# One emission order for all stages of a Sinkhorn-attention, Fourier and MLP kernel, computed by an engine model, with a contiguous K eviction

## The chip, the cores and the metric

One Trainium2 chip, one core. The metric is the device time of one execution in microseconds (us), as the median of several runs. The profiles come from single executions; their span is about 2 us shorter than the device time. Engines: PE is TensorE, DVE is VectorE, ACT is ScalarE, POOL is GpSimd, SP is SyncE. TensorE's clock can be granted in part; 1.00 is full speed, and stretches at 0.5 are called cold. The heads are worked on in pairs ("head pair"), so 4 batches of 8 heads make 16 of them.

## The reference, cut to what matters

```python
# q, k, v: (4 batches, 8 heads, 768, 64) fp32; sort_net: (4, 8, 8, 8)
# moe_w_ch1: (512, 2048), moe_w_ch2: (2048, 512) fp32
P = sort_net
for _ in range(5):                       # Sinkhorn, 8x8 for each batch and head
    P = exp(P - max_row(P)); P = P / sum_row(P); P = P / sum_col(P)
k_sorted = einsum('bhij,bhjcd->bhicd', P, k_blocks)      # mixes 8 blocks of 96 rows
v_sorted = einsum('bhij,bhjcd->bhicd', P, v_blocks)
attn = softmax(q_block @ k_sorted_block.T / 8) @ v_sorted_block   # in each block
x = attn as (4, 768, 512)
u = x + real(fft(fft(x, axis=1), axis=2))
ch = relu(layernorm(u) @ w_ch1) @ w_ch2
out = u + ch
```

The kernel works in fp16 with fp32 accumulation. It writes the softmax as exp(s) - 1 plus a constant part and the Fourier transform as matmuls with cosine and sine tables; one row of it goes through a small fp32 "row path" with a table of its own. The MLP is the larger part of the matmul work.

## The kernel before

The stages were emitted by hand, in an order that mixes batches, so that the MLP of one batch stands beside the attention of another:

```python
    v_mean(0); v_cast(0); attn(0); a_path(0); a_rows(0); a_rows(1); fft_ln(0)
    load_v(1, [nc.sync, nc.sync])        # V of batches 2 and 3
    make_bdk(1); attn(1); fft_ln(1)
    v_mean(1); v_cast(1); v_mix(1); a_path(1)
    mlp(0)
    ...                                  # batches 2 and 3 likewise
    mlp(2); mlp(3)
```

K is mixed on TensorE and evicted by one cast to each of two engines. The mixed rows go out in their natural order, so that neighbouring values of the source land 12 bytes apart:

```python
            dst = ks[:, :, 0:BLK].rearrange("p i (c r) -> p r i c", r=6)[
                :, 3 * half:3 * half + 3]
            src = ps.rearrange("p r (i c) -> p r i c", c=16)
            if half == 0:
                nc.scalar.copy(dst, src)             # L436
            else:
                nc.vector.tensor_copy(dst, src)      # L438
        qr = wt([128, 6, 2, D], F16, "qr", 1)
        nc.vector.tensor_copy(                       # L440: waits for Q's load
            qr, q16[:, 2 * hl:2 * hl + 2].rearrange("p h r d -> p r h d"))
```

The softmax here doesn't subtract the row's maximum and nothing guards it: scores larger than these inputs give would overflow.

## Time and profile before

| | before |
|---|---|
| device time, median | 411.4 us (409.1 to 412.1, 3 runs; a fourth came later) |
| TensorE busy | 316.2 us, 77% of 408.5 |
| first attention scores | 49.1 us |
| first attention times V | 60.3 us |
| first MLP matmul | 121.1 us |

The page of the kernel before. The digits are the busy tenths of 40 slices of 10.2 us each; PEclk is the granted clock, DMA the busy share of the 16 DMA engines. In the stretch view further down this share can pass 1; about 1 and above is read here as full. GB/s counts bytes as they land, after the cast:

```profile
span 408.5 us, 6064 instructions
PE 316.2 (77%) x2452; PEld 185.1 (45%) x2452; DVE 212.2 (52%) x449; ACT 165.7 (41%) x298; POOL 55.7 (14%) x146
PE   0009896686084889989799889798888979979996
PEclk9999997568567999999999999899899989999999
DMA  8989943604030541100101560001000000010202
```

TensorE does nothing in the first three slices, is thin and cold (clock 0.5 to 0.8) in slices 7 to 13, and is dense from 140 us on. The same by stretches, in the stretch view (start and end; length; busy us and instructions of each engine; granted clock; DMA share; GB/s):

```profile
0.00:30.00 30.00, 0.00 (x0) 0.00 (x0) 10.68 (x35) 9.20 (x15) 22.72 (x30) 1.00 0.97 241
30.00:60.00 30.00, 27.65 (x210) 19.80 (x210) 13.26 (x22) 11.77 (x19) 0.75 (x1) 1.00 0.92 206
60.00:100.00 40.00, 28.10 (x267) 20.33 (x268) 26.00 (x55) 17.51 (x28) 2.36 (x3) 0.66 0.39 77
100.00:140.00 40.00, 19.49 (x151) 10.60 (x150) 30.80 (x61) 8.46 (x15) 8.99 (x28) 0.70 0.15 37
140.00:340.00 200.00, 178.55 (x1486) 101.65 (x1484) 119.36 (x257) 95.24 (x176) 18.24 (x71) 0.97 0.16 34
```

Who waits for whom, from the lists of waits of TensorE and VectorE (engine, tile and line, what it waited for: total us, times, longest):

```profile
PE pf_193 L265 <- DVE pdup_189 L256: 30.0, 1, 30.0
PE pf_933 L605 <- DVE un_931 L600: 12.1, 1, 12.1
...
DVE qr_266 L440 <- DMA q_86<-in_q_dram: 14.2, 1, 14.2
```

The first 30 us are a queue fault: VectorE's copy of Q (L440) waits 14.2 us for its load, and the Sinkhorn rounds stand behind it, though they need nothing of Q. GpSimd's timeline (start, length, operation) shows when the weights are loaded:

```profile
2.19 0.75 POOL L138 DMA_DIRECT2D q_86<-in_q_dram  x1
...
22.29 0.74 POOL L219 DMA_DIRECT2D w1sb<-in_moe_w_ch_dram  x1
23.02 1.16 POOL L220 DMA_DIRECT2D w2sb<-in_moe_w_ch_dram  x1
49.79 0.75 POOL L138 DMA_DIRECT2D q_137<-in_q_dram  x1 [25.61 <-DVE qr_518 L440]
```

They are issued at 22.3 us, because memsets stand in front of them in GpSimd's queue (from 2.9 us on, with two loads between them; one memset takes 6.9 us), and, against the program's text, ahead of batch 1's Q, which has to wait for a free buffer.

The K eviction is one line of the groups (busy us of the group, mean ns of one):

```profile
L436 ACT CAST ksb_118<-pf_250 128x384 f16<-128x384 f32 x1 | 1.4, 1442 | 12.0 <-PE pf_250 L427 12.0
```

### The profile page before, as it was taken

The page shows a single profiled execution, that of the slowest core. Times are in us where ns is not written, and L with a number is a line of the kernel's source. Part 1 is how long each engine was busy: PE and PEld are TensorE (multiplying, and loading weights), DVE is VectorE, ACT ScalarE, POOL GpSimd, SP SyncE. Part 2 cuts the span into 40 slices and gives each one's busy share as a digit, 9 for nine tenths or more (in the row PEclk, how much of TensorE's full clock was granted, in tenths as well). Part 3 has the DMA queues.
Part 4 walks back from the last instruction along what each step waited for, and adds up shares of the span by engine and source line. Part 5 has one row for each costly group of instructions (what it writes and reads, how often), then busy time and mean ns, then how long its engine had stood idle before and what let it go on. Part 6 is the DMA issues. An engine that isn't in the chain of part 4 may idle for free.

```text
span 408.5 us, 6064 instructions
## 1 busy us (share of the span) xinstructions
PE 316.2 (77%) x2452; PEld 185.1 (45%) x2452; DVE 212.2 (52%) x449; ACT 165.7 (41%) x298; POOL 55.7 (14%) x146
## 2 busy tenths in 40 slices
PE   0009896686084889989799889798888979979996
PEld 0006484562032555445385545353555535445552
DVE  0272367666785787550475787403686842240101
ACT  3060276711001994124086952150598205224250
POOL 8930000100403110100200100202000020020000
PEclk9999997568567999999999999899899989999999
DMA  8989943604030541100101560001000000010202
GB/s 254 302 166 207 291 98 45 79 10 165 1 103 0 75 61 23 51 26 2 52 27 25 79 100 27 26 2 51 27 2 2 26 26 27 26 53 0 77 2 77
DMA packets 18229, 27.51 MB, mean 67 GB/s; under 512 B 1621, under 2 KB 12569, under 8 KB 18201
## 3 DMA queue, kind: packets, MB, share of 16 engines
q0 software_dynamic: 11040, 10.49, 17.1%
q1 hardware_dynamic: 6872, 15.06, 10.4%
q10 hardware_dynamic: 288, 1.57, 1.1%
q8 instruction: 19, 0.31, 0.3%
q14 instruction: 10, 0.07, 0.1%
HBM read 30.92 MB, written 6.29 MB: 91 GB/s over the span
## 4 chain that ended last, share of the span: by engine, by line
PE 52%; DVE 18%; ACT 13%; DMA 6%; POOL 5%; issue 5%; POOLq 0%; DVEq 0%
DMA q_86<-in_q_dram 4%; PE pf_225 L298 3%; ACT ebuf_114 L476 3%; ACT ebuf_106 L476 2%; DVE ksb_118 L438 1%; PE pf_790 L387 1%; ACT ksb_118 L436 1%; PE pf_206 L278 1%; PE pm_3686 L626 1%; PE pm_4186 L626 1%; PE pm_3840 L626 1%; PE pm_2026 L626 1%; PE pm_2933 L626 1%; PE pm_4167 L626 1%; PE pm_4148 L626 1%
## 5 line engine op out<-in xcount | busy, mean ns | idle before, releaser
L619 PEld LDWEIGHTS <-w1sb 128*128 128x128 f16 x512 | 48.7, 99 | 34.5 <-issue 5.4
L265 PE MATMUL pf_193<-idh_sb,pdup_189 32*128 32x32 f16 x8 | 0.4, 185 | 30.0 <-DVE pdup_189 L256 30.0
L347 PEld LDWEIGHTS <-vcx 128*128 128x128 f16 x128 | 15.6, 187 | 0.1
L265 PEld LDWEIGHTS <-pdup_189 32*128 32x128 f16 x8 | 0.3, 101 | 30.0 <-DVE pdup_189 L256 30.0
L622 ACT ACTIVATE hr_1775<-pm_1776 128x384 f16<-128x384 f32 x1 | 0.5, 491 | 32.2 <-DVE ny_990 L587 32.2
L440 DVE COPY qr_266<-q_86 128x768 f16<-128x768 f16 x1 | 3.3, 3283 | 14.2 <-DMA q_86<-in_q_dram 14.2
L605 PE MATMUL pf_933<-idh_sb,un_931 128*128 128x128 f16 x4 | 0.6, 308 | 12.1 <-DVE un_931 L600 12.1
L491 PEld LDWEIGHTS <-ebuf_110 97*128 97x128 f16 x96 | 5.3, 106 | 8.9 <-DVE ebuf_110 L474 8.9
L491 PEld LDWEIGHTS <-ebuf_102 97*128 97x128 f16 x96 | 5.1, 102 | 8.5 <-DVE ebuf_102 L474 7.2
L350 PEld LDWEIGHTS <-vbn 128*128 128x128 f16 x64 | 8.7, 135 | 0.0
L622 ACT ACTIVATE hr_3743<-pm_3744 128x384 f16<-128x384 f32 x1 | 0.5, 491 | 18.8 <-PE pm_3744 L619 18.8
L233 ACT ACTIVATE pw<-pw 32x64 f32<-32x64 f32 x5 | 1.3, 255 | 15.9 <-DVE pw L240 15.3
L491 PEld LDWEIGHTS <-ebuf_114 97*128 97x128 f16 x96 | 5.5, 108 | 4.8 <-ACT ebuf_114 L476 4.6
L630 DVE TENSOR_TENSOR u_3517<-pm_4148,u_3517 128x512 f32<-128x512 f32 x1 | 0.7, 691 | 13.2 <-PE pm_4148 L626 13.2
L298 PE MATMUL pf_225<-v_78,idf_sb 128*128 128x512 f32 x12 | 7.5, 787 | 0.0
L626 PEld LDWEIGHTS <-hr_1929 128*128 128x128 f16 x48 | 4.7, 98 | 5.6
L626 PEld LDWEIGHTS <-hr_2836 128*128 128x128 f16 x48 | 4.7, 98 | 5.5
L626 PEld LDWEIGHTS <-hr_4051 128*128 128x128 f16 x48 | 4.7, 98 | 5.5
L626 PEld LDWEIGHTS <-hr_3897 128*128 128x128 f16 x48 | 4.7, 98 | 5.5
L626 PEld LDWEIGHTS <-hr_3743 128*128 128x128 f16 x48 | 4.7, 98 | 5.6
L626 PEld LDWEIGHTS <-hr_3589 128*128 128x128 f16 x48 | 4.7, 102 | 5.2 <-issue 0.3
L208 POOL MEMSET vsf<- 1x8192 f16 x1 | 6.9, 6922 | 0.1
(1412 smaller groups left out, 955.5 us busy)
## 6 DMA issues: line engine op xcount, KB each, us to landing
w1sb<-in_moe_w_ch_dram POOLq DMA_DIRECT2D x1, 2048.0 KB, 16.5
w2sb<-in_moe_w_ch_dram POOLq DMA_DIRECT2D x1, 2048.0 KB, 38.6
v_78<-in_v_dram ACTq DMA_DIRECT2D x2, 768.0 KB
v_81<-in_v_dram SPq DMA_DIRECT2D x2, 768.0 KB
v_1034<-in_v_dram SPq DMA_DIRECT2D x2, 768.0 KB, 14.8
v_1037<-in_v_dram SPq DMA_DIRECT2D x2, 768.0 KB, 5.0
tab_775<-k_cd SPq DMA_DIRECT2D x1, 514.0 KB, 14.2
tab_775<-k_sd SPq DMA_DIRECT2D x1, 514.0 KB, 15.8
```

What stands on the lines that cost most here:

```text
L208: nc.gpsimd.memset(vsb[96:97, :, 0:D], 0.0)
L278: nc.tensor.matmul(psv[:, i, :], pv[:, i, :], idf[0:32, 0:32])
L298: nc.tensor.matmul(ps.rearrange("p c d -> p (c d)"), idf, v32[t, n // 6][:, 8 * (n % 6):8 * (n % 6) + 8, :].rearrange("p c d -> p (c d)"), ...
L347: nc.tensor.matmul(ps[:, dd, :], vcx[:, :, d], bd, start=True, stop=(t == 1))
L350: nc.tensor.matmul(ps[:, dd, :], vbn[:, d:d + 1].broadcast_to([128, 128]), bd, start=False, stop=True)
L387: nc.tensor.matmul(psr[64 * o:64 * o + 64, :], atd[:, c].rearrange("p b g i -> p (b g i)"), tab[:, o, c, :], start=(c == 0), stop=(c == 3))
L436: nc.scalar.copy(dst, src)
L438: nc.vector.tensor_copy(dst, src)
L476: nc.scalar.activation(ed, src, AF.Identity, bias=negone[0:96])
L491: nc.tensor.matmul(po[:, 65 * T:65 * T + 96], e[:, S * g + 256 * tt + 128 * n: S * g + 256 * tt + 128 * n + 128], vsf[:, vi:vi + 96], star ...
L619: nc.tensor.matmul(ps, w1sb[:, c, 128 * fc:128 * fc + 128], ut[:, c, :], start=(c == 0), stop=(c == 3))
L626: nc.tensor.matmul(ps, hr[:, fc, 128 * tt:128 * tt + 128], w2sb[:, fc, :], start=(fc == 0), stop=(fc == 15))
```

## The change

The intent, part by part:

- A model of the four compute engines in the emitting program (`op`, `pick`, `evac`) estimates when each result is ready. Stages are generators with priorities, and the one that is ready is emitted. The MLP has the lowest priority and is used as filler.
- A flag has the order of the instructions on each engine computed on a timing simulation before they go to the chip.
- K is evicted contiguously: the rows of a block stay grouped by r, and V is cast into the same order.
- Constant rows (softmax sums, V's row of ones) are loaded and no longer written by GpSimd.
- The row path's table is halved.

```diff
+    ms = tc.block(schedule_with_timeline_sim=True)
+    ctx.enter_context(ms)
...
+    load_qk(0, 0)                        # Q and K of half a batch first
...
         nc.scalar.activation(pw, pw, AF.Exp)
+        if it > 0:
+            v_cast0(it - 1)              # V casts between the Sinkhorn rounds
...
-        t = const.tile([128, NB, 128], F16, name=f"ksb{n}")
+        t = const.tile([128, NB, 8, 16], F16, name=f"ksb{n}")
...
+            t1 = evac(ks[:, :, 3 * half:3 * half + 3, :].rearrange(
+                "p i r c -> p r i c"),
+                ps.rearrange("p r (i c) -> p r i c", c=16), t, 384)
...
+                if (b, hp) == (0, 2):    # weights: emitted at the third head pair
+                    for c in range(4):
+                        nc.gpsimd.dma_start(w1sb[:, c, :], w1v[:, c, :])
+                    for c in range(4):
+                        nc.gpsimd.dma_start(w2sb[:, 4 * c:4 * c + 4, :],
+                                            w2v[:, 4 * c:4 * c + 4, :])
...
+            ut, t = uns[b, g]
+            yield max(t, 62.0)           # the model lets the MLP begin at 62 us
...
-    v_mean(0)
-    v_cast(0)
-    attn(0)
-    ...                                  # the whole order by hand
+    add(0, fft_gen())
+    add(1, a_gen())
+    add(2, attn_gen(k0))
+    add(3, v1_gen())                     # V work of batches 2 and 3, on VectorE
+    add(4, mlp_gen())
+    go()
```

## The prediction

> What bounds the kernel now. The page gives a span of 408.5 us, TensorE busy 316 us (77%), VectorE 212, ScalarE 166. The stretch view divides it:
> - 0 to 30 us: TensorE does nothing. The timeline shows why: VectorE's queue holds a copy of Q (qr) in front of the Sinkhorn loop, and it waits until 17.6 us for its load (14.2 us, the longest wait of VectorE), then takes 3.28 us instead of the usual 0.35 us beside a GpSimd memset of 6.9 us. Sinkhorn then ends at 29.3 us.
> - 60 to 141 us: attention of batch 0, its Fourier stage, and V of batches 2 and 3. TensorE is busy 48.6 of 81 us at a mean granted clock of 0.68. One transpose waits 12.1 us for un.
> - 141 to 408 us: TensorE busy 240 of 267 us, clock 0.97 to 0.99. The remaining holes are transposes at the head of TensorE's queue waiting 2.1 to 2.5 us for un after the rsqrt chain on GpSimd, while MLP work that is ready stands behind them.
>
> TensorE work at full clock, an estimate from dense stretches: MLP 8 x (16 x 0.65 + 3 x 3.45) = 166 us; attention 16 x 2.2 = 35; Fourier and layer norm 4 x 10.6 = 42; V mixing 9.6 + 4; V mean, Sinkhorn transposes and the row path about 17. Together 274 us; the other 134 us are prologue, cold clock, holes and tail.
>
> What the change does.
> 1. Sinkhorn before the Q copy, memsets replaced by loads of constant rows, V casts between rounds, V mean while V lands: TensorE useful from about 17 us (Q still lands near 17 us; the DMA engines are saturated, share about 1). Gain about 15 us net.
> 2. Contiguous K eviction: 32 casts fall from 1.45 to about 0.55 us (a relu eviction of 128x384 takes 0.49): 28 us of VectorE and ScalarE work. The Trainium skill, "SBUF - State Buffer", on 16-byte cachelines, says accesses crossing to a new line pay; the 12-byte stepped write at 1.45 us agrees. On the path: about 1 us per head pair before the MLP.
> 3. Scores of the next head pair before AV, evictions and relus shared between VectorE and ScalarE, layer-norm transposes emitted when due, MLP pieces as filler: the 60 to 141 us stretch shrinks, the 2 us holes fill. The MLP, first seen at 121 us, should start at 62 to 80 us.
> 4. Row path: half the fp32 table matmuls, no table reloads: about 3 us of TensorE, and a DMA wait of 2.5 us.
>
> Sum: 274 - 3 of work, about 10 us of prologue that no work fills, 15 us cold clock and 17 us holes before the MLP starts, 5% of the remaining 215 us, tail 4 us: about 328 us of span. "TensorE: Matmul & The Clock Gate", Part 1, says an idle window re-throttles the clock to half; the trace agrees (0.50 granted from 70 to 80 us).
>
> Predicted: 330 us, range 312 to 354. Chances: faster 0.95, same 0.03, slower 0.02.
>
> What would show it: first TensorE work before 17 us and attention scores by 20 us; K eviction near 0.55 us; first MLP matmul before 80 us; TensorE busy above 85% of the span with clock above 0.95 after 80 us.
>
> What would make it wrong: the simulated order differs from the chip's timing, so an in-order queue again waits at its head; weights landing late; VectorE near 200 us becoming a second limit.

## More of the kernel before

The loads of Q, K and of both MLP weights go through GpSimd's queue and are cast from fp32 to fp16 on the way; V and the tables go through SyncE's. In the program all of batch 0 and 1's Q and K stand before the weights, and GpSimd's memsets before both:

```python
    ...                                  # memsets of ebuf, ksb, vsf, pmt on GpSimd
    load_batch(1)
    nc.gpsimd.dma_start(w1sb, moe_w_ch1.rearrange("(c p) f -> p c f", p=128))
    nc.gpsimd.dma_start(w2sb, moe_w_ch2.rearrange("(c p) m -> p c m", p=128))
```

## The result, and the profile after

| | before | after |
|---|---|---|
| device time, median | 411.7 us (409.1 to 412.2, 4 runs) | 371.8 us (370.9 to 372.3, 4 runs) |
| ratio | | 0.904, 95% interval 0.900 to 0.908 |
| first attention scores | 49.1 us | 31.1 us |
| first attention times V | 60.3 us | 71.8 us |
| first MLP matmul | 121.1 us | 129.6 us |

A ratio here is the mean time of one kernel's fast runs over that of the other's of the same rounds, so it is not quite the ratio of the medians that are quoted. The change is 10% faster, and 42 us slower than the predicted 330. It lies above the range of 312 to 354.

The page after, to be read against that of before (a slice is now 9.2 us):

```profile
span 369.3 us, 6087 instructions
PE 305.4 (83%) x2452; PEld 186.0 (50%) x2452; DVE 220.8 (60%) x507; ACT 138.5 (38%) x249; POOL 43.7 (12%) x155
PE   0989500864885789999998999998999999999995
PEclk9998955775589699999999999999999999999999
DMA  8999987060335100514001101000100100100102
```

```profile
0.00:30.00 30.00, 17.94 (x82) 9.84 (x83) 16.17 (x52) 11.30 (x19) 10.18 (x24) 0.97 1.02 246
30.00:60.00 30.00, 11.81 (x169) 10.42 (x167) 9.73 (x21) 11.86 (x21) 1.48 (x2) 0.73 1.07 235
60.00:100.00 40.00, 25.04 (x268) 19.33 (x268) 28.98 (x57) 16.60 (x31) 2.22 (x3) 0.63 0.26 51
100.00:140.00 40.00, 29.43 (x319) 20.19 (x320) 30.87 (x77) 26.61 (x46) 6.49 (x23) 0.87 0.27 39
140.00:340.00 200.00, 196.06 (x1486) 113.49 (x1485) 123.20 (x283) 71.06 (x132) 23.30 (x104) 1.00 0.12 32
```

Two things are to be seen. From 140 us on, TensorE is 98% busy at full clock (196.06 of 200), where it was 89% busy: the filler works as meant. Before 140 us there is a new hole: from 30 to 60 us TensorE is busy 11.81 us where it had been busy 27.65, while the DMA engines are saturated (share 1.07) and the clock falls to 0.73. The waits name it:

```profile
PE pf_575 L508 <- DMA tab_sb<-k_tab: 23.1, 1, 23.1
PE pm_139 L252 <- DMA v_82<-in_v_dram: 9.8, 1, 9.8
...
DVE qr_207 L271 <- DMA q_72<-in_q_dram: 6.3, 1, 6.3
```

A matmul of the row path stands at the head of TensorE's queue for 23.1 us and waits for its table, from 41.8 to 64.9 us; the last of the V mixing, whose V is there, and with it attention stand behind it. Why the table is late can be read from the two issuing queues. SyncE's timeline (start, length, operation):

```profile
27.77 7.63 SPq L243 DMA_DIRECT2D rb_131<-k_rrow  x1
35.44 1.06 SPq L240 DMA_DIRECT2D lt_133<-k_lt  x1
36.55 14.09 SPq L243 DMA_DIRECT2D rb_135<-k_rrow  x1
50.68 0.34 SPq L144 DMA_DIRECT2D tab_sb<-k_tab  x1
```

and GpSimd's:

```profile
5.31 2.19 POOL L582 DMA_DIRECT2D w1sb<-in_moe_w_ch_dram  x4
7.41 0.84 POOL L584 DMA_DIRECT2D w2sb<-in_moe_w_ch_dram  x1
...
21.79 0.74 POOL L584 DMA_DIRECT2D w2sb<-in_moe_w_ch_dram  x1 [4.60 <-DMA q_123<-in_q_dram]
```

The weights, which the program emits in the third head pair of batch 0 and which nobody needs before the MLP, are issued from 5.3 us on, 17 us earlier than before. The load depends on nothing, so the scheduler moved it up in GpSimd's queue, as it had done in the old kernel; but now the long memsets that used to stand in front of it are gone. They are 8 loads of 512 KB as they land, 4.2 MB, cast from 8.4 MB of fp32 in HBM. What that costs can only be estimated. In the first 60 us 14.4 MB landed (246 and 235 GB/s for 30 us each); by the packed trace 6.9 MB of them came by GpSimd's queue, whose loads here are read at twice that size. That makes some 21 MB read, about 355 GB/s, and for 8.4 MB an estimate of 24 us of all DMA engines.

Meanwhile SyncE's queue falls behind in two ways. Its loads wait, from the ninth on, for the landing of the load eight places before: its list of waits has 2.9 us for `vcx<-k_cdb` and 2.7 us for `vcx<-k_sdb`, each eight places back. And it sits 7.6 and then 14.1 us on the issue of a load of 1 KB. These two are not such waits: the loads eight places before them had landed at 25.4 and 26.9 us. What holds the issue itself is not shown; that it shrinks when the weights go is shown below. The table, the 27th load in this timeline (the texts below count 25), is issued at 50.7 us.

"DMA: Bandwidth & Descriptors" in the Trainium skill, section "Issuing engines are not separate DMA queues", says that loads of all issuing engines run on the same 16 DMA engines and interleave. If so, weights on GpSimd's queue slow the loads on SyncE's; the runs below agree.

The K eviction did what it should (timelines of ScalarE and VectorE):

```profile
27.04 0.48 ACT L163 CAST ksb_107<-pf_209 128x384 f16<-128x384 f32 x1 [0.45 <-PE pf_209 L343]
28.16 0.55 DVE L165 CAST ksb_107<-pf_217 128x384 f16<-128x384 f32 x1
```

### The profile page after: what moved, and what is told of

It is laid out like the page before. It is cut to its first block, busy times and chain, and to the rows that moved or that the text cites. A ratio compares the mean times of both kernels' runs of the same rounds, so it can differ in the third digit from the quotient of the medians.

```text
span 369.3 us, 6087 instructions
## 1 busy us (share of the span) xinstructions
PE 305.4 (83%) x2452; PEld 186.0 (50%) x2452; DVE 220.8 (60%) x507; ACT 138.5 (38%) x249; POOL 43.7 (12%) x155
## 2 busy tenths in 40 slices
DMA packets 18477, 25.95 MB, mean 70 GB/s; under 512 B 1737, under 2 KB 12685, under 8 KB 18449
## 3 DMA queue, kind: packets, MB, share of 16 engines
HBM read 29.37 MB, written 6.29 MB: 97 GB/s over the span
## 4 chain that ended last, share of the span: by engine, by line
PE 57%; DVE 19%; DMA 12%; SPq 7%; issue 2%; ACT 2%; POOL 1%; DVEq 0%; ACTq 0%
SPq L243 6%; DMA vcx<-k_sdb 4%; DMA tab_sb<-k_tab 4%; DMA v_82<-in_v_dram 2%; DVE vcx L873 2%; PE pm_3075 L773 1%; DVE r_540 L425 1%; PE pm_3013 L773 1%; PE pf_575 L508 1%; PE pm_2172 L773 1%; PE pm_2918 L773 1%; PE pm_4212 L773 1%; PE pm_2322 L773 1%; PE pm_3791 L773 1%; PE pm_4039 L773 1%
## 5 line engine op out<-in xcount | busy, mean ns | idle before, releaser
L508 PE MATMUL pf_575<-tab_sb,atp_537 128*64 128x129 f32 (+1 forms) x16 | 3.7, 405 | 23.1 <-DMA tab_sb<-k_tab 23.1
L465 PEld LDWEIGHTS <-vcx 128*128 128x128 f16 x128 | 18.1, 181 | 5.4 <-issue 2.3
L165 DVE CAST vsf<-pm_502 96x512 f16<-96x512 f32 x1 | 0.8, 799 | 27.7 <-PE pm_502 L468 27.7
L508 PEld LDWEIGHTS pf_575<-tab_sb,atp_537 128*64 128x64 f32 x16 | 3.1, 218 | 23.4 <-issue 23.4
L163 ACT CAST vsf<-pm_492 96x512 f16<-96x512 f32 x1 | 0.8, 786 | 25.2 <-PE pm_492 L468 25.2
L252 PEld LDWEIGHTS pm_139<-v_82,idf_sb 128*128 128x128 f32 x12 | 3.1, 267 | 13.6 <-issue 12.5
L773 PEld LDWEIGHTS <-hr_4077 128*128 128x128 f16 x48 | 4.7, 98 | 5.5
L773 PEld LDWEIGHTS <-hr_2224 128*128 128x128 f16 x48 | 4.7, 98 | 5.6
L773 PEld LDWEIGHTS <-hr_3663 128*128 128x128 f16 x48 | 4.7, 98 | 5.5
L773 PEld LDWEIGHTS <-hr_1704 128*128 128x128 f16 x48 | 4.6, 98 | 5.2
L773 PEld LDWEIGHTS <-hr_3127 128*128 128x128 f16 x48 | 4.6, 98 | 5.1
L773 PEld LDWEIGHTS <-hr_3898 128*128 128x128 f16 x48 | 4.6, 98 | 5.1
L692 ACT ACTIVATE un_3291<-u_2960,nm_3108,ny_3106 128x512 f16<-128x512 f32 x1 | 0.8, 813 | 16.8 <-POOL nm_3108 L680 16.8
L368 PEld LDWEIGHTS <-ksb_109 64*128 64x128 f16 x128 | 3.8, 97 | 6.5 <-issue 4.3
L413 PEld LDWEIGHTS <-ebuf_101 97*128 97x128 f16 x96 | 5.7, 108 | 2.6 <-DVE ebuf_101 L390 2.0
L692 ACT ACTIVATE un_2388<-u_2057,nm_2205,ny_2203 128x512 f16<-128x512 f32 x1 | 0.8, 813 | 16.5 <-POOL nm_2205 L680 16.5
L260 ACT CAST vcx<-v_82 128x768 f16<-128x768 f32 x4 | 3.3, 832 | 9.7 <-DMA v_82<-in_v_dram 9.7
L773 PEld LDWEIGHTS <-hr_3365 128*128 128x128 f16 x48 | 4.6, 98 | 4.5
L773 PEld LDWEIGHTS <-hr_2467 128*128 128x128 f16 x48 | 4.2, 98 | 4.7 <-issue 0.2
```

Source lines behind the costliest of these rows:

```text
L252: nc.tensor.matmul(psm.rearrange("p c d -> p (c d)"), idf, v32[n // 6][:, 8 * (n % 6):8 * (n % 6) + 8, :].rearrange("p c d -> p (c d)"), s ...
L260: nc.scalar.copy(vcp[:, 2 * n:2 * n + 2], v32[hf][:, 12 * qq:12 * qq + 12, :].rearrange("p (c r) d -> p c r d", r=6))
L368: nc.tensor.matmul(pss[h2][:, j, :], ks[rows, 4 * g + j].rearrange("p r c -> p (r c)"), qt[rows, :, cc])
L413: nc.tensor.matmul(po[:, 65 * T:65 * T + 96], e[:, S * g + 256 * tt + 128 * n: S * g + 256 * tt + 128 * n + 128], vsf[:, vi:vi + 96], star ...
L465: nc.tensor.matmul(ps[:, dd, :], vcx[:, :, d], bd, start=True, stop=(t == 1))
L508: nc.tensor.matmul(psr[64 * o:64 * o + 64, cs], atp[:, par, c].rearrange("p b g -> p (b g)"), tab[:, o, c, cs], start=(c == 0), stop=(c == 1))
```

## The experiments

The theories after the result are rivals: (A) the table merely stands in the wrong place of SyncE's queue; (B) the early weights take the bandwidth, and whatever is loaded in the first 60 us comes late. (In the text of the second run the weights have 4 MB in HBM; that is their size as they land.) Further questions: what each part of the change is worth alone, and what the rest of the miss is. "First AV" is the first matmul of attention times V.

### Which load is wrong

**Table early.** The table's load moves ahead of V in SyncE's queue.

```diff
     cmh = cload("cmh", [128, 16], F16)
+    tab = cload("tab", [128, 2, 2, 257], F32)     # was: the last of the constants
```

> The changed kernel with the row-path table load moved from 25th in SyncE's queue to 6th, ahead of V. Theory A (place in the queue: the 23.1 us for which TensorE stood in front of the row path is the table's late issue): the stall goes, first MLP matmul about 20 us earlier, 345 to 355 us instead of 371.75. Rival B (the DMA engines are saturated until 60 us, so any load moved forward only pushes another one back): TensorE waits about as long for V or for the second V load, 362 to 374 us.

Measured: 366.6 us (366.6 to 367.8), ratio to before 0.893 (0.889 to 0.896). The wait for the table is gone and 5 us are gained, not 23:

```profile
PE pm L253 <- DMA v<-in_v_dram: 13.9, 2, 11.9
PE pf L414 <- DVE ebuf L391: 12.1, 1, 12.1
PE pf L369 <- DVE qt L359: 8.5, 2, 7.4
```

TensorE now waits 12.1 us and 8.5 us for VectorE, which waits for the second V load (10.9 us) and for Q. The wait has moved from one late load to the next. That speaks against A.

**Weights late.** One value of each weight region is written from the Q of the third head pair first, so that the load can't be issued before that Q is there. The value is then overwritten by the load.

```diff
                 if (b, hp) == (0, 2):
+                    nc.vector.tensor_copy(w1sb[:, :, 0:1], qt[:, 0:4, 0:1])
+                    nc.vector.tensor_copy(w2sb[:, 0:16:4, 0:1],
+                                          qt[:, 0:4, 0:1])
                     for c in range(4):
                         nc.gpsimd.dma_start(w1sb[:, c, :], w1v[:, c, :])
```

> The changed kernel with the MLP weight loads (4 MB in HBM) held until the third head pair's Q of batch 0 is there, by two tiny VectorE copies into the weight tiles; the table load stays 25th. Theory A: the long issue times of the one-row constant loads ahead of the table (7.6 and 14.1 us) belong to those loads and stay; the stall stays near 20 us, 368 to 374 us. Rival B (bandwidth): with 4 MB less in front, SyncE's queue drains sooner, the table lands 12 to 18 us earlier and the stall shrinks to under 8 us, 352 to 362 us.

Measured: 353.6 us (352.5 to 354.1), ratio 0.860 (0.856 to 0.864). 18 us less than the changed kernel. TensorE's wait for the table falls from 23.1 to 1.6 us:

```profile
43.06 1.06 PE L508 MATMUL pf<-tab_sb,atp 128*64 128x129 f32 x8 [1.64 <-DMA tab_sb<-k_tab]
```

SyncE's queue shows why:

```profile
23.48 1.47 SPq L243 DMA_DIRECT2D rb<-k_rrow  x1
24.99 0.44 SPq L240 DMA_DIRECT2D lt<-k_lt  x1
25.48 5.81 SPq L243 DMA_DIRECT2D rb<-k_rrow  x1
31.33 0.34 SPq L144 DMA_DIRECT2D tab_sb<-k_tab  x1
```

The same two issues take 1.5 and 5.8 us, and the table is issued 19 us earlier with its place in the queue unchanged. Nor is it a matter of places in GpSimd's queue: the first K of batch 1 is issued there at 33.9 us (34.3 with early weights), and of the loads before that only one Q comes earlier (11.4 us against 25.2). The first AV comes at 48.1 us (71.8 before this edit), the first MLP matmul at 111.9.

**Both.**

> Table early and weights late together. Theory A alone: same as the table early alone, within 1%. Rival B alone: same as weights late alone. If both act: the second V load lands before 60 us instead of about 73 us, the MLP starts before 100 us, and the time falls to 340 to 350 us. After that the stretch before the MLP should be set by VectorE (busy over 9 tenths from 70 to 110 us in the changed kernel).

Measured: 354.0 us (353.9 to 355.7), the same as with late weights alone. With the weights out of the way, the table's place is worth nothing. B is shown in that the early weights are the cause of 18 us; A's 5 us were a partial repair of the same fault.

### What the parts are worth

**The flag off in the new kernel.**

```diff
-    ms = tc.block(schedule_with_timeline_sim=True)
+    ms = tc.block(schedule_with_timeline_sim=False)
```

> The changed kernel with the timing simulation of the scheduler switched off (the flag alone; the emission order stays). Theory A: the table is still 25th in SyncE's queue and the stall stays; the flag is worth under 2%, 366 to 379 us. Rival C (the simulated order is what helped, or what hurt): more than 3% to one side of 371.75 us.

Measured: 388.5 us (387.7 to 391.6), ratio 0.947 (0.941 to 0.952). TensorE waits 21.4 us in four places for layer-norm rows, beside the table's 20.7. So the flag is worth 17 us in this kernel. And it is not to blame for the weights: without it they are issued from 5.3 to 25.2 us as well, ahead of batch 1's K.

**The flag on in the old kernel.** The same two lines added to the kernel before.

> The kernel before with the timing simulation of the scheduler switched on, nothing else. The flag off cost the changed kernel 4.5% (388.46 against 371.75 us). If the simulated order is worth that by itself, whatever the emission: 388 to 398 us. If it needs the new emission order (pieces to choose among): within 2% of 410 us. In the order that the scheduler writes, the Sinkhorn loop stands mostly ahead of the first Q copy, so TensorE should start before 28 us instead of at 30 us.

Measured: 403.2 us (402.5 to 403.3), ratio 0.983 (0.980 to 0.987). TensorE starts at 22.7 us instead of 30, but then waits 37.8 us in eight places for layer-norm rows. So the flag alone brings under 2% here (the record's verdict, which asks for 2%, is "unclear"; the interval excludes no change). It does not replace the emission order.

**K stepped again in the new kernel.** The old tile form and the old destination, and V cast in the old order, in the changed kernel.

> The changed kernel with the old stepped K eviction (and V in the old order). Each of the 32 casts should take about 1.45 us instead of 0.5. If the prediction's step 2 holds (1 us per head pair before the MLP): 4 to 12 us slower than 371.75, 376 to 384 us. If the casts are off the path in this schedule: within 1%, 368 to 375 us.

Measured: 375.8 us (374.6 to 376.0), ratio 0.915 (0.911 to 0.919), 4 us more than the changed kernel. The casts are back at their old length (groups view):

```profile
L163 ACT CAST ksb<-pf 128x384 f16<-128x384 f32 x22 | 31.7, 1513 | 9.5 <-PE pf L343 9.5
L165 DVE CAST ksb<-pf 128x384 f16<-128x384 f32 x10 | 14.6, 1462 | 2.0 <-PE pf L343 2.0
```

**K contiguous in the old kernel.**

```diff
-            dst = ks[:, :, 0:BLK].rearrange("p i (c r) -> p r i c", r=6)[
-                :, 3 * half:3 * half + 3]
+            dst = ks[:, :, 3 * half:3 * half + 3, :].rearrange(
+                "p i r c -> p r i c")
```

> The kernel before with the contiguous K eviction alone (V in the new order). 32 casts from 1.45 to about 0.5 us, 30 us less engine work. If a quarter lies on the path, as the prediction has it: 399 to 407 us against 410.84 us. If most of it lies on the path (the chain of waits lists both casts again and again during attention): 385 to 398 us.

Measured: 402.8 us (402.4 to 404.9), ratio 0.982 (0.977 to 0.988). The casts take 482 ns on ScalarE and 556 on VectorE. So 30 us of engine time bring 7 us in the old kernel and 4 in the new one, since most casts lie beside the critical path. The length of the casts agrees with "SBUF — State Buffer", its note on SBUF cachelines in the section "Door 1: The DMA port swizzle", by which accesses that cross to a new 16-byte line pay: 12-byte steps took 1.44 to 1.51 us, contiguous runs 0.48 to 0.56. The runs don't separate the crossing of lines from the step as such.

### What the rest of the miss is

With late weights the kernel is still 24 us above the prediction. In that run VectorE is busy 35.9 of the 40 us from 60 to 100, and between 50 and 74 us it does 15 us of V work of batches 2 and 3 (mean, subtraction and cast), which nobody needs until later.

**V work gated.** In addition to late weights, the V work waits for attention of batch 0.

```diff
+        while 0 not in attnd:
+            yield None
+        nc.vector.tensor_copy(
+            vcx[:, 0:96:32, 0:1],
+            rts[0][:, 5:6, DM - 1:DM].broadcast_to([128, 3, 1]))
         for n in range(3):
             while busy():
                 yield None
```

> Weights late (353.64 us), and in addition the VectorE work on V of batches 2 and 3 held behind attention of batch 0 by one tiny copy; nothing is taken away. Theory D (that work, about 16 us and a wait of some 8 us for its load, stands in VectorE's queue in front of attention of batch 0, because the simulated order believed the load to be there): attention of batch 0 ends 10 us or more earlier, 340 to 349 us. Rival F (the stretch before the MLP is set by the attention and layer-norm chain itself): 350 to 358 us.

Measured: 348.9 us (345.2 to 349.1), ratio 0.848 (0.843 to 0.853), 5 us less. Attention of batch 0 ends at 57.5 us instead of 67.7, the 10 us of theory D, but only half of it reaches the end. First MLP matmul at 103.1 us.

**V work off VectorE.** Casts on ScalarE, the mean on TensorE by fp32 identity matmuls as for batches 0 and 1, the mean's correction by 64 more small matmuls; also behind attention of batch 0.

> Weights late, and V of batches 2 and 3 taken off VectorE: its mean by 12 matmuls, its casts on ScalarE, the mean put right by 64 more small matmuls, all held behind attention of batch 0. Theory D: VectorE loses 16 us before the MLP, first MLP matmul before 98 us (111.8 with weights late alone), 330 to 343 us. Rival F: the first MLP matmul stays after 105 us and the time within 2% of 353.64 us; the extra matmuls (about 5 us) may even cost.

Measured: 349.3 us (347.7 to 349.7), the same as gated alone. The fp32 mean is 12 matmuls that TensorE runs as 24 passes of 715 ns mean, 13.3 us of busy time in the groups view, in the middle of the stretch that was to be emptied.

**The same with the mean from the fp16 cast,** 12 one-pass matmuls.

> Weights late; V of batches 2 and 3 off VectorE as in the last try, but its mean from the f16 casts (12 matmuls in one pass) instead of from f32, because the f32 sums stood in TensorE's queue for some 13 us there. Theory D: VectorE loses 16 us before the MLP and TensorE is held under 6 us for it, first MLP matmul before 100 us, 330 to 343 us. Rival F (the stretch is set by the chain of attention, Fourier stage and layer norm, or by the cold clock): within 1.5% of the 348.94 us of the gated kernel. The result stays within the tolerance, if a mean of rounded values is good enough.

Measured: 350.3 us (347.3 to 351.6). VectorE falls to 26.5 of the 40 us, and TensorE now waits 6.8 us for ScalarE's casts. VectorE's load as such is not the limit; the theory that it was, and that 16 us off it would show, fell.

**V loaded straight into its place.** Cast and permuted by its own load on GpSimd's queue, the mean after attention of batch 1, the MLP not waiting for it.

```diff
+        for r in range(6):
+            nc.gpsimd.dma_start(
+                vcx[:, 16 * r:16 * r + 16, :],
+                vv[128:256].rearrange("p (c r) d -> p r c d", r=6)[:, r])
```

> Weights late; V of batches 2 and 3 is cast and put in its place by the load itself, so neither VectorE nor ScalarE touches it, its mean (12 one-pass matmuls) comes after attention of batch 1, and the MLP shares no buffer with it and doesn't wait for it. Theory D2 (in the earlier tries the V work, on whatever engine, stood inside the chain from attention of batch 0 to the first MLP matmul, because the MLP needs its buffers): first MLP matmul before 95 us instead of 103 to 112, time 328 to 340 us. Rival F (the chain of attention, Fourier stage, layer norm, with batch 1's attention mixed in, takes that long anyway): first MLP matmul after 98 us, time 343 to 351 us.

Measured: 352.6 us (349.9 to 353.5, 5 runs), ratio 0.859 (0.857 to 0.861). The load became many small pieces (14,057 packets under 512 bytes; 1,737 in the changed kernel), and the DMA engines moved 179 GB/s in the stretch from 60 to 80 us while full (share 1.90). It gained nothing over the gated kernel. TensorE's longest wait behind the first V load is 6.0 us for layer-norm rows; which of the slower loads cost the rest was not settled.

**Weights one step later,** behind Q and K of batch 1, with V work gated.

```diff
-                if (b, hp) == (0, 2):
+                if (b, hp) == (1, 0):
```

> The gated kernel again (weights late, V work of batches 2 and 3 held behind attention of batch 0), with the weight loads held one step further: behind the Q and K of batch 1 instead of behind the third head pair of batch 0. Measured for the version before it: 348.9 us, first MLP matmul at 103.0 us. Theory L (the loads still stand in the wrong order: batch 1's Q and K wait behind weights that nobody needs yet): attention of batch 1 starts earlier, the first MLP matmul comes before 98 us, 335 to 344 us. Rival F (the chain attention 0, Fourier, layer norm is what keeps the MLP back, on queues that are full of mixed work): first MLP matmul at 100 us or later, 345 to 351 us. If the weights now come too late, the MLP's first matmul waits for their load and the time goes above 351 us.

Measured: 346.5 us (345.2 to 347.6), ratio 0.843 (0.839 to 0.848), first MLP matmul at 105.3 us. Not to be told from the gated kernel (intervals overlap). The order among these loads no longer matters, as the rival expected.

**The prologue as predicted.** The prediction had the first scores by 20 us. In the last kernel they come at 30.7: Q's copy still stands in front of the Sinkhorn rounds, and the rounds wait for the V casts between them. This kernel makes the Q copies wait for Sinkhorn's result and the V casts for the first mixed K, and takes the V mean from the cast.

```diff
+        if (b, hp) in ((0, 0), (0, 1)):
+            nc.vector.tensor_copy(qr[0:32, 0, 0, 0:1], pw[:, 0, 0:1])
...
-        if it > 0:
-            v_cast0(it - 1)
...
+    nc.scalar.copy(vcp[0:32, 0:16:2, 0, 0:1], k0[0][0][0:32, :, 0, 0:1])
+    for n in range(8):
+        v_cast0(n)
```

> The last kernel (weights behind batch 1's Q and K, V work of batches 2 and 3 gated; 346.5 us) with the prologue that the prediction assumed: the two Q copies and the eight V casts can no longer be placed between the Sinkhorn rounds (they wait for its result and for the first mixed K), and the V mean of batches 0 and 1 is taken from the fp16 cast in one-pass matmuls after the first scores, so that it doesn't stand in front of K mixing. In the kernel before it Sinkhorn ends at 23.3 us, K mixing starts at 26.2 and the first scores at 30.7. Theory P (the prologue is one of the mis-sized terms, and its delay runs through to the end): Sinkhorn ends at 13 to 15 us, first scores at 17 to 20 us, first MLP matmul at 93 to 99 us, 335 to 342 us. Rival L (loads bound the first stage, so an early start only waits later: V of batches 0 and 1 lands at 20.7 us and the table at 43 us whatever the order): scores come at 17 to 20 us too, but the V mixing still ends near 33 us or later, first MLP matmul at 102 us or later, 344 to 350 us.

Measured: 355.3 us (354.6 to 356.1), ratio 0.865 (0.862 to 0.867): 9 us slower. TensorE's timeline:

```profile
15.27 0.85 PE L340 MATMUL pf<-bdk,k 128*64 128x128 f16 x12 [0.93 <-DVE bdk L318]
18.53 0.82 PE L365 MATMUL pf<-qt,ksb 64*128 64x96 f16 x16 [1.65 <-ACT vcx L260]
...
45.73 2.01 PE L505 MATMUL pf<-tab_sb,atp 128*64 128x129 f32 x12 [7.92 <-DMA tab_sb<-k_tab]
```

The prologue is now just what was predicted: K mixing at 15.3 us, scores at 18.5. But the row path has moved forward too and stands at the head of the queue for 7.9 us until its table lands, with the rest of the V mixing behind it. First AV at 56.0 us.

**The same prologue in the changed kernel as it is.**

> The same new prologue in the changed kernel as it is (weights early, V work ungated; 371.8 us). Both theories expect first scores before 21 us. If the loads bound the first 65 us there, the table still lands near 65 us and the gain is swallowed: 368 to 373 us. If the prologue's delay is additive, 359 to 365 us.

Measured: 375.8 us (374.7 to 376.6), ratio 0.914 (0.910 to 0.917): 4 us slower than the changed kernel, and above both expectations. The wait for the table grew from 23.1 to 27.4 us: an early start only waits longer.

**Early prologue and early table,** with late weights and gated V work.

> The kernel with the early prologue and late weights (355.3 us; scores at 18.5 us, then 7.9 us of TensorE waiting for the cosine table with the rest of the V mixing behind it, first MLP matmul at 111.3 us), with the table's load put early in SyncE's queue, ahead of the V pieces. Theory P (the early prologue is worth its 11 us once no table is in the way): no wait for the table, attention of batch 0 ends before 52 us, first MLP matmul at 92 to 99 us, 334 to 342 us. Rival L (the loads as a whole bound the first stage): the 0.5 MB of table push the V pieces and batch 1's loads back by some 2 us, the wait moves to V or to batch 1's Q and K, first MLP matmul at 100 us or later, 344 to 352 us.

Measured: 346.2 us (346.1 to 347.0), ratio 0.841 (0.838 to 0.845). Scores at 18.5 us, no wait for the table, first AV at 46.3 us against 48.2, first MLP matmul at 103.6. Twelve microseconds at the start became two at the first AV. Attention times V needs all of V mixed; the V casts run until 23.2 us, and the 64 mixings, which begin at 29.4, and their evictions follow. Scores were never on that path. The run doesn't tell whether V's loads or the mixing itself sets the 46 us. That the loads alone do, as the rival had it, is not shown.

**No V work of batches 2 and 3 at all.** On the gated kernel; wrong for batches 2 and 3, whose mixing reads stale values.

```diff
-    v1_load()
...
+        vbs[1] = vbs[0]          # in place of the sums, the mean and the subtraction
```

> Wrong on purpose for batches 2 and 3: the gated kernel (348.9 us, first MLP matmul at 103.0 us, VectorE busy 35.3 of the 40 us from 60 to 100) without the load of V of batches 2 and 3 (3.1 MB) and without its work on VectorE (16 us); their V mixing reads the values that are there from batches 0 and 1. Theory V (this load and this work, in the middle of the stretch before the MLP, are what keeps the MLP back): first MLP matmul before 92 us, 328 to 337 us. Rival F (the chain attention 0, Fourier, layer norm, mixed with attention of batch 1 in the queues, sets it): first MLP matmul at 97 us or later, 340 to 348 us.

Measured: 337.1 us (335.0 to 337.4), ratio 0.819 (0.815 to 0.823), 12 us less than the gated kernel. From 60 to 100 us, the gated kernel and then this one:

```profile
60.00:100.00 40.00, 26.34 (x267) 17.77 (x268) 35.25 (x75) 22.71 (x40) 6.64 (x20) 0.76 0.66 101
```

```profile
60.00:100.00 40.00, 28.93 (x352) 20.01 (x349) 29.82 (x76) 27.03 (x50) 6.27 (x19) 0.83 0.56 83
```

TensorE gets through 352 matmuls instead of 267. The first MLP matmul comes at 100.1 us, only 3 us earlier. So both theories were half right. This load (3.1 MB) and its work cost about 12 us, and the MLP's start is not where they are felt: TensorE has other work to fill with when V doesn't have to be waited for.

**Attention of batch 1 later.** On the gated kernel, with the V work in it.

```diff
     def attn(b, pre=None):
+        while b == 1 and (0, 0) not in uns:
+            yield None
```

> The gated kernel with one wait in the emission: attention of batch 1 is not emitted before the first layer-norm half of batch 0 has its transposes. Everything else as it was, V work of batches 2 and 3 included. Theory F (attention of batch 1, emitted at a higher priority, fills the queues between attention 0 and the MLP): first MLP matmul at 78 to 92 us, and the whole 330 to 343 us if the MLP then fills TensorE, though attention of batch 1 comes later. Theory V: VectorE's V work stays in the way, first MLP matmul at 97 us or later, 345 us or more. If only the order changes and not the amount of waiting, the first MLP matmul comes early and the time stays at 345 to 352 us.

Measured: 357.7 us (356.6 to 359.8), ratio 0.871 (0.865 to 0.876), 9 us slower, though the first MLP matmul came at 95.7 us, the earliest of all. In its list of waits TensorE stands 13.0 us for V of batches 2 and 3 and has no attention to fill with. So the start of the MLP, which the prediction used as its measure, is a poor one: what counts is work in TensorE's queue that doesn't wait.

## Why the prediction was wrong

Direction and order of size were right, the size was not: 371.8 us, predicted 330, range 312 to 354. Point by point:

- **Work after the MLP starts ("5% of the remaining 215 us", tail 4): right.** From 140 to 340 us TensorE was 98% busy at clock 1.00.
- **Step 2, contiguous K eviction: right.** Predicted 1.45 to 0.55 us; measured 0.48 to 0.55. Alone it is worth 7 us in the old kernel and 4 in the new.
- **Step 4, the row path: its matmuls were looked at, its load was not.** The prediction counted on a 2.5 us DMA wait going away. The path's own table became the largest wait of the new kernel, 23.1 us.
- **Step 3 failed: "the 60 to 141 us stretch shrinks ... The MLP, first seen at 121 us, should start at 62 to 80 us".** It started at 129.6 us, later than before. What stood in its place was a wait at the head of TensorE's in-order queue, 23.1 us for the table that the early weights had made late, and behind it V work of batches 2 and 3. With the weights late that wait is 1.6 us and the MLP starts at 111.9 us; in no run did it start before 95.7. Of the terms "about 10 us of prologue that no work fills, 15 us cold clock and 17 us holes before the MLP starts", the prologue and the holes, 27 us together, were mis-sized; the clock was not (see below). The span less the 271 us of work in the prediction's sum leaves 98 us (an estimate, since the 271 are one); of these the prediction placed 57. The missing 41 lie before 140 us, for after it TensorE idles only 8 us. One thing stays open here: TensorE's busy time is 305.4 us and not 271, of which some 16 are cold clock (below). Whether the work was estimated short or the modelled ends of the matmul records make it long, the runs don't say.
- **Where the 42 us went,** by the runs: 18 us to the weights, issued at 5.3 us (354 without that); 5 us to V work of batches 2 and 3 in front of attention of batch 0 (349); about 12 us more to that V work and its load (337 without it). As that result is wrong, the 12 us are what leaving them out brings and no correct version was shown to save them. The remaining 7 us to 330 have no shown cause.
- **Step 1, the prologue: the prediction's timing was missed (first scores at 31.1 us and not by 20), but that is not a cause.** With the predicted prologue the kernel was no faster (346.2 against 346.5 us), or slower.

The prediction named the mechanism among what could make it wrong ("an in-order queue again waits at its head; weights landing late"), but gave it no time. It had noted that the DMA engines are saturated in the first stage, and used that for Q alone. It listed "memsets replaced by loads of constant rows" as a gain, and did not ask what those memsets had been holding back: an engine off the critical path, GpSimd, had set when the weights' load began. And it feared only "weights landing late", as their new place in the program, the third head pair, suggests, although the profile of before already showed them issued ahead of batch 1's Q. It was their earliness that cost.

The clock term held. "TensorE: Matmul & The Clock Gate", Part 1, has the clock halve after an idle window of about 3.4 us; the trace agrees: TensorE goes idle at 41.8 us, and by the trace's clock record 0.5 is granted from 45.2 to 69.1 us, 4 us into the work that follows. (The place that the prediction gives, 70 to 80 us of the kernel before, shows the half clock but not the idle window: 0.5 begins there at 65.4 us, after a gap of 1.9 us. The 12.1 us wait at 100.7 us shows it, with 0.5 from 102.9.) An estimate from the stretch view, busy time times the missing clock share: 11.81 x 0.27 + 25.04 x 0.37 + 29.43 x 0.13 = 16 us. That is close to the 15 predicted, and to the 15 of the kernel before by the same sum (28.10 x 0.34 + 19.49 x 0.30). The clock was not the error; the waits were.

What stays open: whether the 12 us of V work of batches 2 and 3 are its load, its time on VectorE or the order around it. The run that took it away took all three. What holds SyncE 7.6 and 14.1 us on the issue of 1 KB while the weights load is open too. No correct version below 346 us was found; the best are the last kernels with late weights and gated V work (346.2 and 346.5 us, not to be told apart), 16% faster than before and 7% faster than the change as it was.

## What to carry to other kernels

When work is taken off an idle-looking engine, ask which loads stood behind it in its queue: they will start earlier and may take the bandwidth of loads that are needed first. Give each large load that isn't needed yet a dependence that says when it may start, and add up what must land before the first stage can run against the rate that the trace shows, for loads that cast in bytes before the cast. When one wait at the head of an in-order queue is removed, look at once for the next one behind it: the first fix here brought 5 of 23 us, and the fix of the cause 18. Judge an order by how much ready work each queue holds, not by how early a chosen stage begins.

## What the Trainium skill lacked or had wrong

- "DMA: Bandwidth & Descriptors", "Issuing engines are not separate DMA queues", calls the time to initiate a DMA usually small relative to the DMA. Under saturation it was not: SyncE stood 7.63 and 14.09 us on the issue of two loads of 1 KB, and 1.47 and 5.81 us once 4.2 MB of other traffic were moved away. Neither was a wait for an earlier load (those had landed at 25.4 and 26.9 us); what holds the issue is not said there.
- "DMA: Bandwidth & Descriptors", Bandwidth, gives 341 GB/s for transfers of 1 MB and Specifications about 358 as a core's limit. This case was full (share 1.02 to 1.07) at 235 to 246 GB/s, but that is no contradiction: the profile counts bytes as they land, 25.95 MB over the run, of which 6.29 MB are output, while 29.37 MB were read from HBM, since the loads on GpSimd's queue halve their bytes. Counted before the cast the first 60 us come to the 355 GB/s estimated above. What the page lacks is a word on which side of a cast its rates count.
- "TensorE: Matmul & The Clock Gate", Part 1, puts the ramp penalty below 1% of a typical span. That is one warm-up; the same part goes on to show that waits make it recur, and so it is here: the estimate above is 16 us of 369, about 4%. The page is not wrong, but the 1% is easily taken alone.
- No page that I read for the prediction says that an engine's own work in front of a load in its queue acts as a throttle on the load. Here memsets on GpSimd had held the weights (4.2 MB as they land) back until 22.3 us; without them the weights left at 5.3 us and cost 18 us.
